# Four tokens to a row for r at the start of a fused RWKV and squared-ReLU kernel

## The chip, the cores and the metric

The kernel runs on one core of a Trainium2 chip. The metric is the device time of one execution in microseconds. Most executions of one kernel agree within 0.3%.

## The reference

Inputs are `r`, `k`, `v` of shape (4 batches, 8 heads, 768 tokens, 48), `w` and `u` of shape (8, 48), and two weight matrices of 384x2048 and 2048x384, all float32. A linear recurrence runs over the tokens, and its result goes through a two-layer network with a squared ReLU:

```python
state = zeros((B, H, D, D))
for t in range(S):
    kt, vt, rt = k[:, :, t], v[:, :, t], r[:, :, t]
    cur = einsum('bhd,bhe->bhde', u[None] * kt, vt)
    y[:, :, t] = einsum('bhd,bhde->bhe', rt, state + cur)
    state = w[None, :, :, None] * state + einsum('bhd,bhe->bhde', kt, vt)
x = y.transpose(0, 2, 1, 3).reshape(B * S, H * D)
out = (maximum(x @ w_in, 0) ** 2) @ w_out
```

## The kernel before

The work is cut into 24 units: 6 chunks of 128 tokens times 4 batches, chunk by chunk, so units 0 to 3 are the first chunk. For each unit the kernel loads r, k and v with the 128 tokens on the partitions (`load`, line 278; tiles `ldr`, `ldk`, `ldv`), scales r by a power of w that depends on the token and k by the inverse power (`scale`, line 300, on DVE; tile `rkw`), turns both so that the features lie on the partitions (`turn` and `evict_rk` through PE and ACT for units 0 to 5, `turn_dma` for the others), multiplies them into two 128-token score matrices (`at`, line 337), masks these (`mask`, line 349, on DVE), and forms y from the masked scores and the running state (`y_mm`, lines 400 and 406). `sums` adds the outer products of k and v and the diagonal term with u; `diag_v` and `evict_y` bring the diagonal term and y together. y is turned (`x_turn` with `evict_x`, or `x_dma`) and goes through `mm1` (line 447), `relu`, `square` and `mm2` (line 471); `evict_o` and `store` write it out.

The powers of w come from a spread of log w to all partitions (`spread_log`, PE, out of the one-row tile `wrow`), and an exponential with one exponent for each partition (`power`, ACT). `spread_columns` and `copy_columns` bring w and u to columns, from which `u_columns` and `end_columns` make small constants on POOL. `fill` is a matmul of constants whose result nobody reads.

Nothing is ordered by a scheduler at run time. A list of words, `SCHEDULE`, says in which order the steps are issued; each step appends its instructions to its engines' queues, and every engine works its own queue in order. A number behind `@` is the PSUM bank of the step, and `3*fill` is three fills. The loads of units 2 to 5 go to POOL's DMA queue, together with the two weight matrices, each in four quarters (`weights`, lines 285 to 291); the other loads, and the transposes by DMA, go to SP's. The first quarter of w_in waits on POOL for k of unit 0, by a small copy into `gate`. Buffers for the loads are handed out in the order of the list from pools of 3 (r), 8 (k) and 4 (v). The list starts:

```python
load:0:kt fill@0 load:0:rt 2*fill load:1:rt 2*fill load:1:kt fill columns 2*fill spread_log@1 load:0:vt load:2:rt
load:1:vt weights:kt.0:0:I fill power:0 3*fill load:2:kt power:1 scale:0:0 load:6:kt fill spread_columns@2 scale:1:0
load:2:vt fill load:9:kt scale:0:1 2*fill copy_columns turn:0:0@3 load:3:rt fill evict_rk:0:0 turn:0:1@4 u_columns
```

Of the kernel before, what the change touches and what calls it, by code (L numbers as in the profile page):

```python
# [8 lines left out]
F32 = mybir.dt.float32  # L9
BF16 = mybir.dt.bfloat16  # L10
AF = mybir.ActivationFunctionType
# [6 lines left out]
load:0:kt fill@0 load:0:rt 2*fill load:1:rt 2*fill load:1:kt fill columns 2*fill spread_log@1 load:0:vt load:2:rt  # L18
load:1:vt weights:kt.0:0:I fill power:0 3*fill load:2:kt power:1 scale:0:0 load:6:kt fill spread_columns@2 scale:1:0
load:2:vt fill load:9:kt scale:0:1 2*fill copy_columns turn:0:0@3 load:3:rt fill evict_rk:0:0 turn:0:1@4 u_columns  # L20
fill evict_rk:0:1 fill scale:2:0 turn:1:0@5 load:3:kt fill rk:0 at:0@6,7 scale:1:1 weights:-:1:I fill mask:0:0 fill
turn:1:1@1 cast_v:0 weights:-:2:I mask:0:1 fill evict_rk:1:0 fill load:7:kt fill load:3:vt evict_rk:1:1 y_mm:0@2
2*fill sums:0@3 load:4:rt fill diag_v:0 turn:2:0@4 end_columns rk:1 at:1@6,7 evict_rk:2:0 evict_y:0 2*fill scale:2:1
2*fill x_turn:0@5 mask:1:1 6*fill mask:1:0 3*fill turn:2:1@1 scale:3:0 fill weights:-:3:I evict_rk:2:1 3*fill
scale:3:1 2*fill evict_x:0 fill turn:3:0@4 load:5:rt rk:2 cast_v:2 fill at:2@2,7 load:6:rt fill mask:2:0 fill
weights:-:0:O fill mm1:0:1:0@6 state_add:0 load:4:kt turn:3:1@1 relu:0:1:0 3*fill mask:2:1 fill cast_v:1 mm1:0:1:1@5
weights:-:1:O evict_rk:3:0 sums:1@2 state_cast:0 fill load:4:vt diag_v:1 sums:2@3 y_mm:1@6 relu:0:1:1 y_mm:2@7
evict_y:1 fill mm1:0:1:2@4 evict_rk:3:1 load:5:vt diag_v:2 fill rk:3 x_turn:1@5 at:3@6,1 evict_x:1 evict_y:2
load:5:kt fill relu:0:1:2 fill mask:3:0 3*fill cast_v:3 mm1:1:1:1@5 square:0:1:1:0 square:0:1:0:1 load:8:kt sums:3@7
mask:3:1 x_turn:2@4 mm1:1:1:0@6 evict_x:2 diag_v:3 relu:1:1:1 y_mm:3@1 state_add:1 weights:-:2:O mm1:2:1:2@4  # L30
relu:1:1:0 square:0:1:2:1 evict_y:3 mm1:2:1:1@5 square:1:1:0:1 state_add:3 weights:-:3:O mm1:2:1:0@6 state_add:2
x_turn:3@2 fill evict_x:3 mm1:2:1:3@1 scale:4:0 relu:2:1:2 fill mm1:1:1:3@7 relu:2:1:1 square:2:1:2:1 square:2:1:1:0
mm1:0:1:3@3 relu:2:1:0 mm1:3:1:1@2 square:2:1:0:1 mm1:3:1:3@4 relu:3:1:1 scale:4:1 mm2:1:0@5 square:1:1:1:1
relu:1:1:3 turn:4:0@6 mm2:0:0@2 relu:0:1:3 load:7:rt mm1:1:1:2@7 relu:2:1:3 evict_rk:4:0 fill turn:4:1@3 fill
mm1:3:1:0@1 evict_rk:4:1 cast_v:4 rk:4 mm2:1:1 scale:5:0 relu:1:1:2 at:4@6,0 relu:3:1:0 mm2:2:0@3 mask:4:1
state_cast:2 turn:5:0@7 mask:4:0 sums:4@1 square:1:1:2:1 mm2:0:1 scale:5:1 evict_rk:5:0 diag_v:4 y_mm:4@0 mm2:2:1
evict_y:4 turn:5:1@6 scale:6:1 mm2:0:2 evict_rk:5:1 state_add:4 square:3:1:0:1 x_turn:4@7 mm2:2:2 square:0:1:3:0
evict_x:4 square:3:1:1:1 at:5@0,6 load:6:vt mm2:3:0@1 state_cast:3 mask:5:1 mm1:4:1:0@7 square:1:1:3:0 load:8:rt
state_cast:1 rk:5 mm2:3:1 cast_v:5 mask:5:0 relu:3:1:3 mm2:0:3 square:2:1:3:0 mm1:4:1:3@6 scale:6:0 mm2:2:3
relu:4:1:3 turn_dma:6 relu:4:1:0 sums:5@0 y_mm:5@4 diag_v:5 mm1:4:1:2@6 load:8:vt scale:7:1 evict_y:5 mm1:4:1:1@7  # L40
relu:4:1:2 scale:7:0 square:4:1:0:1 mm2:1:2 state_decay:4 turn_dma:7 square:4:1:3:0 x_turn:5@4 mm2:1:3 evict_x:5
square:3:1:3:0 relu:4:1:1 mm2:4:0@6 load:7:vt evict_o:0 square:4:1:1:0 mm1:5:1:3@4 store:0:POOL load:9:rt scale:8:0
mm2:4:1 relu:5:1:3 scale:8:1 load:10:rt evict_o:1 rk:6 at:6@7,2 square:4:1:2:1 mm1:5:1:1@4 mask:6:1 cast_v:6
turn_dma:8 mm1:5:1:0@5 mask:6:0 relu:5:1:1 state_add:5 mm2:4:2 relu:5:1:0 square:5:1:1:1 mm1:5:1:2@2 sums:6@4
relu:5:1:2 mm2:4:3 diag_v:6 square:5:1:0:1 state_decay:5 y_mm:6@7 cast_v:7 rk:7 at:7@5,0 evict_y:6 square:5:1:2:1
mm2:5:0@2 mask:7:1 x_dma:6 mm1:3:1:2@7 state_add:6 mm2:5:1 relu:3:1:2 load:10:kt mask:7:0 load:9:vt sums:7@0
square:3:1:2:1 scale:9:1 mm2:5:2 evict_o:4 diag_v:7 y_mm:7@4 state_cast:4 store:4:POOL scale:9:0 at:8@7,5 evict_y:7
cast_v:8 turn_dma:9 mm2:3:2 store:1:POOL rk:8 mm1:6:1:0@6 square:5:1:3:0 x_dma:7 scale:10:0 sums:8@4 relu:6:1:0
mm2:5:3 state_add:7 mm1:6:1:1@6 evict_o:5 load:11:kt state_decay:6 square:6:1:0:1 mask:8:1 load:11:rt mm1:6:1:3@0
state_cast:5 scale:10:1 mm2:6:0@2 mask:8:0 state_cast:6 mm2:3:3 diag_v:8 turn_dma:10 relu:6:1:1 y_mm:8@5 relu:6:1:3  # L50
mm1:6:1:2@7 evict_y:8 cast_v:9 square:6:1:1:0 x_dma:8 at:9@6,0 relu:6:1:2 mm1:7:1:1@5 rk:9 square:6:1:2:1
square:6:1:3:0 sums:9@7 load:12:rt evict_o:2 mm2:6:1 mask:9:1 relu:7:1:1 load:10:vt store:2:POOL mask:9:0 mm2:6:2
# [505 lines left out]
```

## Time and profile before

| | |
|---|---|
| median of 3 runs | 177.45 us (177.1 to 177.91) |
| the profiled execution's own time | 176.95 us |
| its span, first to last instruction | 175.1 us |
| PE, DVE, ACT, POOL busy | 167.7, 128.8, 128.1, 33.2 us |
| fills on PE | 68 |
| DMA moved | 28.83 MB, mean 165 GB/s |
| packets under 512 B | 89681 of 93848 |

PE is TensorE's matmuls, PEld its weight loads, DVE VectorE, ACT ScalarE, POOL GpSimd, SP SyncE. The ends of matmuls are modelled and overlap the next one, so a busy PE is not PE at its peak. The granted clock is 1.00 in every stretch of the trace. SP's queue is `q1`, POOL's is `q0`, and `q10` carries the one load that ACT issues, that of w.

### The profile page before, as it was taken

The page shows a single profiled execution, that of the slowest core. Times are in us where ns is not written, and L with a number is a line of the kernel's source. Part 1 is how long each engine was busy: PE and PEld are TensorE (multiplying, and loading weights), DVE is VectorE, ACT ScalarE, POOL GpSimd, SP SyncE. Part 2 cuts the span into 40 slices and gives each one's busy share as a digit, 9 for nine tenths or more (in the row PEclk, how much of TensorE's full clock was granted, in tenths as well). Part 3 has the DMA queues.
Part 4 walks back from the last instruction along what each step waited for, and adds up shares of the span by engine and source line. Part 5 has one row for each costly group of instructions (what it writes and reads, how often), then busy time and mean ns, then how long its engine had stood idle before and what let it go on. Part 6 is the DMA issues. An engine that isn't in the chain of part 4 may idle for free.

```text
span 175.1 us, 4846 instructions
## 1 busy us (share of the span) xinstructions
PE 167.7 (96%) x1946; PEld 132.1 (75%) x1946; DVE 128.8 (74%) x280; ACT 128.1 (73%) x266; POOL 33.2 (19%) x66
## 2 busy tenths in 40 slices
PE   7869999999999999999999999999999999999992
PEld 3547999777787888696786886986886886878870
DVE  4459797199788998997998999689988497550400
ACT  4344798977787797799486989299498595992951
POOL 8998560000010203000201101010110011120010
PEclk9999999999999999999999999999999999999999
DMA  5999999978595999999999998998999987521013
GB/s 109 196 221 191 215 231 249 197 139 160 108 217 106 193 159 215 198 196 155 178 236 170 230 118 188 205 131 190 207 172 170 161 165 201 112 78 35 4 45 135
DMA packets 93848, 28.83 MB, mean 165 GB/s; under 512 B 89681, under 2 KB 91730, under 8 KB 93826
## 3 DMA queue, kind: packets, MB, share of 16 engines
q1 hardware_dynamic: 89472, 18.88, 63.5%
q0 software_dynamic: 4352, 9.64, 22.7%
q8 instruction: 15, 0.25, 0.6%
q14 instruction: 7, 0.06, 0.2%
q10 hardware_dynamic: 2, 0.00, 0.0%
HBM read 20.45 MB, written 4.72 MB: 144 GB/s over the span
## 4 chain that ended last, share of the span: by engine, by line
PE 76%; DMA 9%; ACT 6%; DVE 4%; SPq 2%; issue 1%; DVEq 0%
PE bank L447 31%; PE bank L471 30%; DMA ldv<-in_v_dram 4%; PE bank L337 4%; DMA rkT<-rkw 3%; PE bank L245 2%; PE bank L400 2%; PE bank L362 2%; ACT gr L455 2%; DMA xT<-yb 2%; SPq L278 2%; PE bank L406 2%; PE bank L486 2%; ACT g L462 1%; DVE g L464 1%; ACT osb L478 1%
## 5 line engine op out<-in xcount | busy, mean ns | idle before, releaser
L447 PE MATMUL bank<-xT,w_in_q 128*128 128x128 bf16 (+1 forms) x768 | 72.4, 246 | 0.3 <-DMA xT<-yb 0.3
L455 ACT ACTIVATE gr<-bank 128x512 f32<-128x512 f32 x96 | 53.7, 603 | 20.2 <-PE bank L447 18.9
L471 PE MATMUL bank<-w_out_q,g 128*128 128x384 bf16 x368 | 68.5, 326 | 0.0
L447 PEld LDWEIGHTS <-w_in_q 128*128 128x128 bf16 x768 | 64.1, 114 | 3.6 <-issue 0.5
L471 PEld LDWEIGHTS <-g 128*128 128x128 bf16 x368 | 33.5, 98 | 18.4
L462 ACT ACTIVATE g<-gr 128x512 bf16<-128x512 f32 x60 | 37.0, 641 | 0.4
L505 POOL DMA_DIRECT2D out_dram<-osb x21 | 11.3, 542 | 131.5 <-ACT osb L478 120.3
L349 DVE TENSOR_TENSOR am<-bank,smask 128x512 bf16<-128x512 f32 x48 | 31.5, 683 | 1.9 <-PE bank L337 1.5
L464 DVE TENSOR_TENSOR g<-gr 128x512 bf16<-128x512 f32 x36 | 24.5, 685 | 9.9 <-ACT gr L455 9.7
L371 DVE TENSOR_TENSOR dv<-vb,bank 128x384 f32<-128x384 bf16 x24 | 13.2, 549 | 7.5 <-PE bank L362 4.6
L300 DVE TENSOR_TENSOR rkw<-ldr,wpos 128x384 bf16<-128x384 f32 x24 | 13.2, 551 | 5.2 <-DMA ldr<-in_r_dram 2.6
L415 DVE TENSOR_TENSOR yb<-bank,dv 128x384 bf16<-128x384 f32 x24 | 13.3, 554 | 4.8 <-PE bank L406 4.1
L391 ACT CAST stb<-st 64x192 bf16<-64x192 f32 x40 | 13.9, 349 | 2.4 <-DVE st L385 2.0
L304 ACT CAST vb<-ldv 128x384 bf16<-128x384 f32 x24 | 12.3, 513 | 3.8 <-DMA ldv<-in_v_dram 3.5
L478 ACT COPY osb<-bank 128x384 f32<-128x384 f32 x23 | 11.0, 486 | 5.5 <-PE bank L471 5.4
L245 PE MATMUL bank<-warm 128*128 128x256 bf16 x68 | 13.6, 315 | 1.2 <-DVE warm L193 1.2
L329 DVE TENSOR_TENSOR rk<-rkT 128x512 bf16<-128x512 bf16 x24 | 10.0, 419 | 5.8 <-ACT rkT L324 4.3
L300 DVE TENSOR_TENSOR rkw<-ldk,wneg 128x384 bf16<-128x384 f32 x24 | 13.2, 550 | 0.3 <-DMA ldk<-in_k_dram 0.3
L381 DVE TENSOR_TENSOR st<-bank,st 64x192 f32<-64x192 f32 x32 | 11.2, 351 | 0.2
L324 ACT COPY rkT<-bank 128x512 bf16<-128x512 bf16 x12 | 6.9, 585 | 6.0 <-PE bank L320 5.9
L400 PE MATMUL bank<-vb,am 128*128 128x48 bf16 x192 | 8.6, 183 | 1.4 <-ACT vb L304 1.4
L400 PEld LDWEIGHTS <-am 128*128 128x128 bf16 x192 | 7.8, 96 | 2.6 <-issue 1.4
(61 smaller groups left out, 115.6 us busy)
## 6 DMA issues: line engine op xcount, KB each, us to landing
out_dram<-osb POOLq DMA_DIRECT2D x21, 192.0 KB, 3.3
ldk<-in_k_dram SPq DMA_DIRECT2D x20, 192.0 KB, 4.0
ldr<-in_r_dram SPq DMA_DIRECT2D x20, 192.0 KB, 4.1
ldv<-in_v_dram SPq DMA_DIRECT2D x20, 192.0 KB, 4.0
w_in_q<-in_moe_w_in_dram POOLq DMA_DIRECT2D x4, 384.0 KB, 8.6
w_out_q<-in_moe_w_out_dram POOLq DMA_DIRECT2D x4, 384.0 KB, 11.4
ldr<-in_r_dram POOLq DMA_DIRECT2D x4, 192.0 KB, 8.4
ldk<-in_k_dram POOLq DMA_DIRECT2D x4, 192.0 KB, 8.7
```

Of the source, the lines that this page charges most:

```text
L245: nc.tensor.matmul(out=bank("fill")[:, :WIDE], lhsT=warm[:, :128], rhs=warm, start=True, stop=True)
L300: nc.vector.tensor_tensor(t["rkw"][:, x, :, :, :D], pair(src), pair(wx), ALU.mult)
L349: nc.vector.tensor_tensor(am, t["at"][o], smask.unsqueeze(1).to_broadcast([C, HP, C]), ALU.mult)
L371: nc.vector.tensor_tensor(t["dv"], t["vb"], t["d"].unsqueeze(2).to_broadcast([C, H, D]), ALU.mult)
L391: nc.scalar.copy(stb[b][sl, :, o * D : (o + 1) * D], st32[b][sl])
L400: nc.tensor.matmul(out=y[:, 2 * p + o, :], lhsT=t[f"am{o}"][:, p, :], rhs=t["vb"][:, 2 * p + o, :], start=(o == 0 and p == 0), stop=c == 0 ...
L415: nc.vector.tensor_tensor(t["yb"], t["y"], t["dv"].rearrange("p h d -> p (h d)"), ALU.add)
L447: nc.tensor.matmul(out=t["h", s][:, a], lhsT=turned, rhs=chunks[c]["xT"][:, n, b : b + m, :], start=(n == 0), stop=(n == NK - 1),)
L455: nc.scalar.activation(t["gr", s], t["h", s], AF.Relu)
L462: nc.scalar.activation(g, x, AF.Square)
L464: nc.vector.tensor_tensor(g, x, x, ALU.mult)
L471: nc.tensor.matmul(out=t["o"], lhsT=chunks[units[i][0]]["g"][:, f, units[i][1], :], rhs=w_out_q[f // 4][:, f % 4, :], start=(f == 0), stop ...
```

## The change

- **r of units 0 to 5.** A row of the tile is now four tokens of one head. Each load is two transfers, one for the even heads and one for the odd: partition 32a + s holds tokens 4s to 4s + 3 of head 2a + o. `scale` multiplies with a table in the same order (`packed_pos`), and `evict_rk` puts the tokens back into their order while it copies out of PSUM.
- **w.** It is loaded as four rows (`w4`) rather than one, and its logarithm is spread from these: once for the packed table (`spread_log:0`, then four exponentials of 96 columns, `power:0`), once for the plain tables (`spread_log:1`, `power:1`, and `power:2` later). The columns of w are copied from `w4` on DVE instead of being loaded again; u's load moves to SP.
- **Weights.** Each quarter comes in two pieces, and the pieces alternate on POOL's queue with r, k and v of units 1 to 5. The copy that made the first quarter wait for k of unit 0 is gone.
- **Engines and order.** `u_columns`, `end_columns` and a memset move from POOL to DVE; the two 128x128 constant masks stay on POOL but move behind the first loads of the list; v of unit 1 moves from SP to POOL. The pools are 5, 6 and 5 buffers. The whole list is in a new order.

The diff, without most of the list:

```diff
+load:0:kt fill@0 load:1:rt triangle 3*fill load:2:rt fill load:0:rt 3*fill identity copy_w spread_log:0@1 load:1:kt
+load:3:rt columns fill power:0 spread_log:1@2 load:0:vt weights:2:I:0 load:2:kt scale:0:0 fill power:1 fill
+scale:1:0 weights:0:I:1 2*fill scale:0:1 fill turn:1:0@3 load:1:vt load:6:rt scale:1:1 fill turn:0:0@4 scale:2:0
+weights:2:I:1 fill evict_rk:0:0 fill turn:0:1@5 scale:3:0 load:3:kt fill evict_rk:0:1 turn:1:1@6 evict_rk:1:0
+load:4:rt fill rk:0 at:0@7,1 evict_rk:1:1 fill load:5:rt mask:0:0 fill spread_columns@4 load:6:kt mask:0:1
+weights:3:I:1 fill cast_v:0 scale:2:1 2*fill load:2:vt at:1@5,3 copy_columns rk:1 u_columns fill cast_v:1
+weights:0:I:0 fill end_columns sums:0@6 load:4:kt mask:1:1 y_mm:0@7 fill turn:2:0@1 diag_v:0 fill evict_rk:2:0 fill
+weights:1:I:1 fill load:7:kt fill mask:1:0 fill turn:2:1@4 power:2 sums:1@3 load:3:vt load:8:rt scale:3:1 fill
+evict_rk:2:1 3*fill y_mm:1@1 evict_y:0 2*fill weights:1:I:0 at:2@5,2 diag_v:1 fill mask:2:0 fill weights:3:I:0 fill
+x_turn:0@4 turn:3:0@7 evict_x:0 evict_y:1 2*fill load:4:vt fill evict_rk:3:0 2*fill mask:2:1 2*fill cast_v:2 3*fill
+state_add:0 weights:2:O:1 3*fill x_turn:1@5 fill evict_x:1 y_mm:2@4 load:5:kt rk:2 turn:3:1@1 scale:4:0 fill
+evict_rk:3:1 mm1:0:1:0@7 weights:1:O:0 scale:5:0 sums:2@2 relu:0:1:0 scale:4:1 turn:4:0@6 weights:0:O:0 fill
...
-    wrow = const.tile([1, dm], F32)
-    nc.scalar.dma_start(out=wrow, in_=w.rearrange("h d -> (h d)").unsqueeze(0))
+    J = 4
+    w4 = const.tile([HP, 2, D], F32)
+    nc.scalar.dma_start(out=w4, in_=w.rearrange("(p o) d -> p o d", o=2))
...
+    select = const.tile([HP, HP, 32], F32)
+    nc.vector.tensor_copy(select, ident4.unsqueeze(2).to_broadcast([HP, HP, 32]))
+    spread_p = const.tile([HP, HP, 128], F32)
+    nc.vector.tensor_copy(spread_p, ident4.unsqueeze(2).to_broadcast([HP, HP, 128]))
+    shift = const.tile([128, J], F32)
+    for n in range(4):
+        for j in range(J):
+            nc.vector.memset(shift[32 * n : 32 * n + 32, j : j + 1], float(j - C * n - C // 2))
+    packed_up = const.tile([128, J], F32)
+    nc.vector.scalar_tensor_tensor(packed_up, iota_i.to_broadcast([128, J]), float(J), shift, ALU.mult, ALU.add)
...
+        if x == 0:
+            for j in range(J):
+                nc.scalar.activation(
+                    packed_pos[:, j].rearrange("p o d -> p (o d)"), spread["log", 0][:, : 2 * D], AF.Exp,
+                    scale=packed_up[:, j : j + 1],
+                )
...
-        (nc.gpsimd if i in (2, 3, 4, 5) else nc.sync).dma_start(
-            out=x, in_=src[b, :, c * C : (c + 1) * C, :].rearrange("h s d -> s h d")
-        )
+        queue = nc.gpsimd if i in (2, 3, 4, 5) or name + str(i) in ('vt1',) else nc.sync
...
+        if name == "rt" and i < NPE:
+            for o in range(2):
+                queue.dma_start(
+                    out=x[:, o * J : (o + 1) * J, :].rearrange("p j d -> p (j d)"),
+                    in_=src.rearrange("(a o) (s j) d -> o a s (j d)", o=2, j=J)[o],
+                )
+        else:
+            queue.dma_start(out=x, in_=src.rearrange("h s d -> s h d"))
...
-    def weights(after, q, which):
-        if after is not None:
-            nc.gpsimd.tensor_copy(gate, tiles[after[1]][after[0]][:, 0, :1])
+    def weights(q, which, part):
         if which == "I":
...
+            sl = slice(0, 2) if part == 0 else slice(2, NK)
+            nc.gpsimd.dma_start(out=w_in_q[q][:, sl, :], in_=src[:, sl, q * dff // NQ : (q + 1) * dff // NQ])
...
-        nc.scalar.copy(t["rkT"][:, x], t["tp", x])
+        if x == 0:
+            nc.scalar.copy(
+                t["rkT"][:, 0].rearrange("q a (s j) -> q a s j", j=J), t["tp", 0].rearrange("q j (a s) -> q a s j", a=HP)
+            )
+        else:
+            nc.scalar.copy(t["rkT"][:, 1], t["tp", 1])
```

More of the change, by code (lines that the diff above doesn't have):

```diff
@@ L17 @@
 SCHEDULE = """
[L18 to L52, printed above, removed]
@@ L145 @@
     const = ctx.enter_context(tc.tile_pool(name="const", bufs=1))
[L146 to L148 removed]
+    room = {'ldr': 5,
+            'ldk': 6,
+            'ldv': 5,
             'rkw': 4,
```

221 lines of the change are left out of this document (128 added, 93 removed).

## The prediction

> **What bounds the kernel now.** I read the page first, then the stages, PE's waits and the start instruction by instruction.
>
> ```profile
> span 175.1 us, 4846 instructions
> PE 167.7 (96%) x1946; PEld 132.1 (75%) x1946; DVE 128.8 (74%) x280; ACT 128.1 (73%) x266; POOL 33.2 (19%) x66
> ...
> PE   7869999999999999999999999999999999999992
> ...
> DMA  5999999978595999999999998998999987521013
> ```
>
> From the third slice on, PE has no visible hole until the last one. The stages of the start say more:
>
> ```profile
> 0.00:4.00 4.00, 2.75 (x10) 1.53 (x10) 2.17 (x18) 1.80 (x2) 3.20 (x15) 1.00 0.53 100
> 4.00:8.00 4.00, 3.46 (x17) 1.89 (x16) 1.66 (x4) 1.05 (x2) 4.00 (x6) 1.00 1.13 197
> 8.00:12.00 4.00, 3.08 (x31) 2.12 (x29) 2.69 (x5) 1.28 (x3) 3.89 (x8) 1.00 1.22 230
> 12.00:16.00 4.00, 3.23 (x48) 2.58 (x48) 2.59 (x6) 1.96 (x4) 3.44 (x10) 1.00 1.16 179
> 16.00:20.00 4.00, 4.00 (x60) 3.53 (x58) 3.70 (x8) 2.44 (x6) 3.55 (x5) 1.00 1.22 209
> ```
>
> The columns are PE, PEld, DVE, ACT and POOL busy, granted clock, DMA share and GB/s. PE is full from 16 us, and the DMA engines are full (share above 1) from 4 us on. What PE does before 16 us is mostly fill:
>
> ```profile
> 9.75 0.40 PE L337 MATMUL bank<-rkT 64*128 64x128 bf16 x8
> ...
> 15.00 1.15 PE L245 MATMUL bank<-warm 128*128 128x256 bf16 x9
> ...
> 18.06 0.83 PE L447 MATMUL bank<-xT,w_in_q 128*128 128x128 bf16 x12
> ```
>
> The row at 9.75 is `at:0`, the one at 18.06 the first `mm1`, 8.3 us later. Nine fills take 1.15 us, one of them 0.27 in flight, so a fill costs (1.15 - 0.27)/8 = 0.11 us. Since PE does not stop after about 16 us, the whole time is the moment of the first `mm1`, plus the PE work that still stands behind it, plus the waits there. That is my sum. The PE waits of the first 40 us are short:
>
> ```profile
> PE bank L400 <- ACT vb L304: 1.4, 1, 1.4
> ...
> PE bank L258 <- DMA wu<-in_w_dram: 0.5, 1, 0.5
> ```
>
> So the waits that a better start could take away come to 1.9 us in these two. The profiled execution took 176.95 us, 1.85 outside its span; the median of the runs is 177.45, 0.5 above it. I make the sum as a difference and add it to the median.
>
> **The change, part by part.** *PE work behind the first `mm1`.* Both lists hold 68 fills and the same matmuls of weight size. Counted in the two lists, 52 fills stand ahead of the first `mm1` before and 56 after, and `turn:3:1`, `y_mm:1`, `y_mm:2`, `sums:1` and `x_turn:1` move ahead of it.
>
> ```profile
> 14.82 0.34 PE bank L431 x3
> ...
> 16.14 0.22 PE bank L320 x4
> ...
> 20.31 0.19 PE bank L362 x4
> ...
> 20.88 0.40 PE bank L400 x16
> ```
>
> A turn is 0.22, two y products 0.40, sums about 0.2 to 0.3, x_turn below 0.34: about 1.0 us, and four fills 0.44. So the first `mm1` may come 1.5 us later at no cost: term one, -1.5.
>
> *The r loads.* Before, a load is 1024 runs of 192 B, with the 128 tokens as the outermost extent on both sides. After, each r load of units 0 to 5 is two transfers of 128 runs of 768 B, whose source counts 4 pairs of heads, then 32 rows. How a transfer is dealt to engines decides its price. The trace has both ends:
>
> ```profile
> q1 hardware_dynamic: 1743, 0.33, 108.4%
> ...
> q10 hardware_dynamic: 2, 0.00, 3.4%
> ```
>
> The first row is the window 2.2 to 3.8 us, where only SP's 128-row loads run: all 16 engines busy, 1.6 x 16 x 1.084 / 1743 = 16 ns for a 192 B packet. The second is 1.60 to 1.75 us, the load of `wrow`, whose outermost extent is one: two packets, so one of data on one engine (the other marks the end), 0.15 x 16 x 0.034 = 0.08 us for 1.5 KB. The engines used follow the outermost extent at both ends. A half of r has an outermost extent of 4 on one side; I take four engines for it, 24.6 KB on each. At `wrow`'s rate a half is 1.3 us, at the 192 B rate (128 x 16 ns) 2.0 us, and if it did spread over sixteen it would be a quarter of these or less, 0.3 to 0.5. I take 1.3, the row with the longer run. Nothing in this trace shows whether successive transfers on SP take the same four engines; I take that they do. The Trainium skill (DMA: Bandwidth & Descriptors, Rules for kernel authors, "Use all 16 engines") says so: the engine count comes from the slowest dimension larger than one, and an outermost extent below 16 confines the transfer to that many. By the same page's section on why a DMA increments its semaphore by 16, SP's queue always takes the lowest-numbered ones, so these four halves would run one after the other; no run here shows that yet.
>
> What they stand behind and in front of on SP's queue:
>
> ```profile
> L278 SPq DMA_DIRECT2D ldk<-in_k_dram x1: 457/457/457, 0.7 to 0.7; - x1
> DMA to landing us min/median/max: 3.1/3.1/3.1
> ...
> L278 SPq DMA_DIRECT2D ldr<-in_r_dram x2: 567/682/797, 1.3 to 1.9; - x2
> DMA to landing us min/median/max: 3.9/4.1/4.2
> ...
> L278 SPq DMA_DIRECT2D ldk<-in_k_dram x1: 1305/1305/1305, 2.7 to 2.7; - x1
> DMA to landing us min/median/max: 4.8/4.8/4.8
> ...
> L278 SPq DMA_DIRECT2D ldv<-in_v_dram x1: 706/706/706, 4.1 to 4.1; - x1
> DMA to landing us min/median/max: 7.8/7.8/7.8
> ```
>
> Before: k0 lands at 3.8, r0 at 5.2, r1 at 6.1, k1 at 7.5, v0 at 11.9. v0 came 4.4 us after k1, although the earlier loads follow each other by 1.0 to 1.4: sharing with POOL's r2 and weights cost it 3. After, the order is k0, r1, r0, k1, u, v0. Four halves at 1.3 put r0 at 3.8 + 5.2 = 9.0 and k1 at 10.0 if nobody else were there; POOL, now without the copy that held its weights for k0, feeds r2, r3 and pieces of w_in into the same engines from about 4 us. With some 2 of v0's 3 us, k1 lands at 12. Bounds: 6.5 (sixteen shares, half price) to 14.
>
> *From k1 to `at:0`.* `at:0` now stands behind `turn:1:1` on PE, which needs `scale:1:1`, which needs k1. That is a scale and a turn with hand-over: 12 + 0.55 + 0.6 gives `at:0` at 13.2 against 9.75. Everything behind `scale:0:0` and `scale:1:1` on DVE waits with them (the scales of units 2 and 3, the masks), and `load:4:rt` on POOL waits for r1's buffer, with the weights behind it. In the other bound DVE's four scales in a row from 5.4 put `at:0` at 9.2.
>
> *From `at:0` to the first `mm1`.* DVE has in this stretch six masks, two scales, two dv, two yb, one rk, and a copy of the columns, then ten small operations that POOL did before.
>
> ```profile
> 5.42 0.56 DVE L300 TENSOR_TENSOR rkw<-ldr,wpos 128x384 bf16<-128x384 f32 x1 [2.39 <-ACT wpos L253]
> ...
> 7.09 0.16 DVE L261 COPY cols<-bank 128x8 f32<-128x8 f32 x1
> ...
> 10.25 1.29 DVE L349 TENSOR_TENSOR am<-bank,smask 128x512 bf16<-128x512 f32 x2
> 13.41 0.55 DVE L371 TENSOR_TENSOR dv<-vb,bank 128x384 f32<-128x384 bf16 x1 [1.87 <-ACT rkT L324]
> 13.88 0.42 DVE L329 TENSOR_TENSOR rk<-rkT 128x512 bf16<-128x512 bf16 x1
> 14.21 0.55 DVE L415 TENSOR_TENSOR yb<-bank,dv 128x384 bf16<-128x384 f32 x1
> ...
> L218 DVE MEMSET rkw<- 128x64 uint32 x8 | 0.6, 112 | 0.0
> ...
> L291 POOL DMA_DIRECT2D w_out_q<-in_moe_w_out_dram x4 | 2.3, 567 | 1.2 <-DMA w_in_q<-in_moe_w_in_dram 1.0 <-issue 0.2
> ```
>
> That is 6 x 0.645 + 6 x 0.55 + 0.42 + 0.16 + 10 x 0.13 = 9.05 us; the small ones lie between 0.08 (eight memsets in 0.6) and 0.16 (the copy). With `y_mm:2`, `turn:3:1`, a fill and hand-overs (0.8) it is 9.9 against 8.3 before: +1.6, bounds +1.1 to +2.0. Term two is then (13.2 - 9.75) + 1.6 = +5.1.
>
> *At nothing.* The sixteen one-column memsets, the two copies of the small identity and the packed exponents add about 2 us to DVE's preparation, covered by r0's landing; in the sixteen-share case they end about when the four 96-column exponentials do. The 96-column spreads replace one of 384 at the same total. The reordered copy out of PSUM reads 128x512 as before; I keep ACT's price and bound it by twice, hidden while ACT waits for PE. The sixteen memsets are priced by the eight above. The weight pieces add eight POOL issues of 0.57 us (the last row), under the transfers already queued. The new buffers and the reordering after 40 us I count as +0.4 between -1 and +1.5, since PE had no slack to gain there.
>
> Sum: -1.5 + 5.1 + 0.4 = +4.0, so 181.5 us.
>
> **The rivals.** *The packing works as meant.* The halves spread over sixteen engines (or over different fours at once), k1 lands at 6.5, `at:0` at 9.2, and POOL's load of v1 ends the late v. Then -0.55 + 1.1 - 1.5 and a start without the late vb (up to 1.4 of waiting) give about -1.2: 176.2. For it: 768 B runs cut 1024 packets to 256 where the DMA share is above 1. The same page of the skill, in its specifications, wants runs of at least 512 B for line rate, which would favour this case. Against it: the row of `wrow`. It decides from r0 and r1 landing by about 6. *Starved.* r0 and k1 get through only once POOL's queue has run dry at `load:4:rt`, held for r1's buffer: k1 at 16 rather than 12, 185.5. For it: v0's 7.8. *Hidden.* Four engines, but at half price and with little sharing, k1 at 9.5: 2.5 less at `at:0`, and the smaller prices of the small operations (-0.5) and no loss later (-0.4) leave +0.6; with the late vb gone (-0.4) it is 177.6.
>
> **How the numbers follow.** Four engines with sharing 0.62; works as meant 0.18; starved 0.10; hidden 0.10. About 0.5% is what a measurement of this kernel tells from no change. Faster is the second case, 0.18; same is the last, 0.10; slower the other two, 0.72. Four shares with k1 between 10 and 14 give 179.5 to 183.5, with the other bounds 178 to 185. The range leaves out the case that works as meant and the end of the starved one, and takes in the hidden one: 176.8 to 186.
>
> **What would show it.** In the profile after: the r loads on SP landing at 7 us or later where they took 4.1; DVE's first scale waiting for ldr, not for the exponentials; PE idle before its first turn; `at:0` near 13, the first `mm1` near 23; DVE gapless from there; the load of w, now four rows, leaving a few packets on its queue, not 16 or more; PE full from then on. I am wrong if the scale of unit 0 starts before 6.5 us, or if the time lost at the first `mm1` is given back behind it.

## The result, and the profile after

| | before | after |
|---|---|---|
| median | 177.33 us (177.1 to 177.91, 4 runs) | 188.62 us (188.32 to 189.8, 4 runs) |
| ratio | | 1.0644 [1.0591, 1.0696] |
| profiled execution, span | 176.95, 175.1 us | 188.6, 186.8 us |
| `scale:0:0` / `at:0` / first `mm1` start at | 5.42 / 9.75 / 18.06 us | 15.66 / 19.63 / 30.64 us |
| span behind the first `mm1` | 157.0 us | 156.2 us |

Medians are of all executions of a run; a ratio leaves out those more than 1.5% above the fastest of their kernel.

The change makes the kernel slower by 6.4%. The forecast was slower by 2.3%, 181.5 us; the measured time lies above its range. The page of the changed kernel:

```profile
span 186.8 us, 4913 instructions
...
PE   7504799999999999999999979999999999999992
...
PEclk9999969999999999999999999999999999999999
DMA  2996999994079996999996999699999796622023
```

A slice is 4.7 us. PE now has a hole in the second, third and fourth slices, where the kernel before had one shallow start; from the sixth slice on the two are alike. The stretches of the start show what stood still (columns as in the prediction):

```profile
8.00:12.00 4.00, 0.00 (x0) 0.00 (x0) 0.00 (x0) 0.00 (x0) 1.95 (x3) 1.00 1.20 221
12.00:16.00 4.00, 0.00 (x0) 0.00 (x0) 0.34 (x1) 0.00 (x0) 0.00 (x0) 1.00 0.78 159
16.00:20.00 4.00, 3.25 (x29) 2.65 (x29) 3.08 (x7) 1.70 (x4) 3.48 (x6) 1.00 0.74 146
20.00:24.00 4.00, 2.76 (x43) 1.90 (x38) 3.52 (x14) 1.27 (x3) 3.35 (x5) 0.91 1.32 186
24.00:28.00 4.00, 4.00 (x46) 3.19 (x45) 3.56 (x9) 1.65 (x3) 3.35 (x5) 0.66 1.20 224
```

From 8 to nearly 16 us PE, DVE and ACT do nothing at all, while the DMA share is 1.20 from 8 to 12. The engines wait for data, and the DMA engines move mostly other data. Which data DVE waits for stands in its timeline:

```profile
3.97 0.13 DVE L254 COPY wu<-w 4x96 f32<-4x96 f32 x1
15.66 1.03 DVE L341 TENSOR_TENSOR rkw<-ldr,packed_pos 128x384 bf16<-128x384 f32 x2 [11.56 <-DMA ldr<-in_r_dram]
...
17.31 0.56 DVE L341 TENSOR_TENSOR rkw<-ldk,wneg 128x384 bf16<-128x384 f32 x1 [0.15 <-DMA ldk<-in_k_dram]
...
22.31 0.16 DVE L297 TENSOR_TENSOR cols<-cols 128x4 f32<-128x4 f32 x1
22.50 0.45 DVE L300 CAST uwb<-cols 64x4 bf16<-64x4 f32 x2
22.97 0.16 DVE L303 TENSOR_TENSOR wend_c<-cols 128x4 f32<-128x4 f32 x1
23.17 1.15 DVE L305 TENSOR_TENSOR wend_c<-wend_c 128x4 f32<-128x4 f32 x6
```

The bracket is the idle time before the instruction and what ended it: 11.56 us for r. The scale at 17.31 is `scale:1:1`; k1 landed only then. The chain of work that ended last puts the same 12 us on one transfer (start, duration, what):

```profile
3.19 12.35 DMA ldr<-in_r_dram
```

PE's timeline has the two marks of the sum, and fills that cost twice what they did:

```profile
16.75 0.61 PE L361 MATMUL bank<-identb,rkw 128*128 128x128 bf16 x4 [9.55 <-DVE rkw L341]
...
19.63 0.49 PE L383 MATMUL bank<-rkT 64*128 64x128 bf16 x8
...
20.60 0.50 PE L263 MATMUL bank<-warm 128*128 128x256 bf16 x3
...
24.20 1.27 PE L263 MATMUL bank<-warm 128*128 128x256 bf16 x5
...
30.64 0.83 PE L493 MATMUL bank<-xT,w_in_q 128*128 128x128 bf16 x12
```

The span grew by 11.8 us: 10.2 at the first scale, -0.4 from there to `at:0` (3.97 against 4.33), 2.7 from `at:0` to the first `mm1` (11.01 against 8.31), -0.8 behind it. A single fast fill shows 0.27 and a slow one 0.42 in flight. So the three fills at 20.60 cost (0.50 - 0.27) / 2 = 0.115 us each, about as before, and the five at 24.20 cost (1.27 - 0.42) / 4 = 0.21, where the granted clock is low. PE's longest waits:

```profile
PE bank L361 <- DVE rkw L341: 9.6, 1, 9.6
PE bank L403 <- DVE uwb L300: 1.2, 1, 1.2
PE bank L493 <- DMA xT<-yb: 1.2, 2, 1.1
```

### The profile page after: what moved, and what is told of

Read it like the earlier page. It is cut to its first block, busy times and chain, and to the rows that moved or that the text cites. A ratio compares the mean times of both kernels' runs of the same rounds, so it can differ in the third digit from the quotient of the medians.

```text
span 186.8 us, 4913 instructions
## 1 busy us (share of the span) xinstructions
PE 170.2 (91%) x1954; PEld 135.4 (72%) x1954; DVE 132.0 (71%) x310; ACT 128.9 (69%) x270; POOL 36.2 (19%) x65
## 4 chain that ended last, share of the span: by engine, by line
PE 83%; DMA 11%; DVE 3%; SPq 1%; issue 1%; ACT 0%; DVEq 0%
PE bank L493 34%; PE bank L517 29%; DMA ldr<-in_r_dram 7%; PE bank L383 4%; DMA xT<-yb 4%; PE bank L263 4%; PE bank L446 3%; PE bank L361 2%; PE bank L408 2%; PE bank L452 2%; PE bank L532 1%; PE bank L403 1%; SPq L314 1%; DVE am L395 1%; DVE yb L461 1%
## 5 line engine op out<-in xcount | busy, mean ns | idle before, releaser
L517 PE MATMUL bank<-w_out_q,g 128*128 128x384 bf16 x368 | 67.0, 326 | 0.0
L517 PEld LDWEIGHTS <-g 128*128 128x128 bf16 x368 | 34.1, 98 | 19.2
L395 DVE TENSOR_TENSOR am<-bank,smask 128x512 bf16<-128x512 f32 x48 | 32.3, 686 | 7.1 <-PE bank L383 6.7
L508 ACT ACTIVATE g<-gr 128x512 bf16<-128x512 f32 x60 | 36.3, 637 | 0.5
L263 PE MATMUL bank<-warm 128*128 128x256 bf16 x68 | 15.5, 331 | 1.2 <-DVE warm L196 1.2
L361 PE MATMUL bank<-identb,rkw 128*128 128x128 bf16 x48 | 6.1, 266 | 9.6 <-DVE rkw L341 9.6
L366 ACT COPY rkT<-bank 128x512 bf16<-128x512 bf16 x6 | 3.5, 590 | 14.6 <-PE bank L361 14.6
L361 PEld LDWEIGHTS <-rkw 128*128 128x128 bf16 x48 | 4.5, 122 | 10.5 <-DVE rkw L341 10.0
L341 DVE TENSOR_TENSOR rkw<-ldr,packed_pos 128x384 bf16<-128x384 f32 x6 | 3.1, 553 | 11.6 <-DMA ldr<-in_r_dram 11.6
```

The source lines that it names most:

```text
L263: nc.tensor.matmul(out=bank("fill")[:, :WIDE], lhsT=warm[:, :128], rhs=warm, start=True, stop=True)
L341: nc.vector.tensor_tensor(t["rkw"][:, x, :, :, :D], a, b, ALU.mult)
L361: nc.tensor.transpose(t["tp", x][:, p, :], t["rkw"][:, x, p].rearrange("p o e -> p (o e)"), identb)
L395: nc.vector.tensor_tensor(am, t["at"][o], smask.unsqueeze(1).to_broadcast([C, HP, C]), ALU.mult)
L508: nc.scalar.activation(g, x, AF.Square)
L517: nc.tensor.matmul(out=t["o"], lhsT=chunks[units[i][0]]["g"][:, f, units[i][1], :], rhs=w_out_q[f // 4][:, f % 4, :], start=(f == 0), stop ...
```

## The experiments

All times in the table are from the profiled execution but the median and its ratio to the kernel before. The span behind the first `mm1` is 155 to 158 us in every run, so a run is decided mostly by what its start does.

| run | first scale | `at:0` | first `mm1` | span | median | ratio, 95% |
|---|---|---|---|---|---|---|
| before | 5.42 | 9.75 | 18.06 | 175.1 | | |
| after | 15.66 | 19.63 | 30.64 | 186.8 | 188.62 | 1.0644 [1.0591, 1.0696] |
| r0, r1 in four transfers of extent 32 | 9.17 | 13.14 | 25.16 | 181.8 | 184.47 | 1.039 [1.0313, 1.0466] |
| POOL's weights held for r0 | 12.08 | 16.05 | 29.26 | 187.5 | 189.38 | 1.069 [1.0639, 1.0741] |
| no packing, rest kept | 7.17 | 11.14 | 21.68 | 178.4 | 180.52 | 1.0201 [1.0145, 1.0256] |
| all r in four transfers | 6.76 | 10.74 | 26.81 | 183.6 | 186.12 | 1.0506 [1.0432, 1.058] |
| tokens outermost (4s + a) | 7.07 | 11.04 | 21.28 | 177.5 | 179.35 | 1.0132 [1.0103, 1.0161] |
| the same, three list edits | 4.99 | 10.48 | 24.12 | 179.3 | 181.02 | 1.0214 [1.019, 1.0238] |
| all POOL loads held for r0 | 9.56 | 15.22 | 31.23 | 189.3 | 191.08 (one run) | |
| no packing, columns on POOL | 6.22 | 10.20 | 24.79 | 181.0 | 181.87 | 1.0263 [1.0242, 1.0283] |
| tokens outermost, r0 first | 5.02 | 10.15 | 21.55 | 177.4 | 178.9 | 1.0093 [1.0062, 1.0124] |
| the same, columns later | 5.14 | 10.49 | 21.34 | 177.5 | 179.08 | 1.0119 [1.0075, 1.0162] |
| the same, r2 held | 4.85 | 9.90 | 24.51 | 181.2 | 183.0 | 1.0325 [1.0296, 1.0355] |
| r0 first, weight piece 0:I:0 earlier | 5.14 | 10.42 | 22.53 | 178.2 | 179.85 | 1.0151 [1.0133, 1.0169] |
| the same, `y_mm:2` behind | 5.06 | 10.86 | 20.91 | 176.7 | 178.51 | 1.0073 [1.0048, 1.0099] |
| r0 first, `y_mm:2` behind alone | 5.17 | 11.05 | 22.94 | 178.9 | 179.88 | 1.0139 [1.0094, 1.0184] |
| kernel before, packed with 4s + a | 4.86 | 9.75 | 17.12 | 175.0 | 176.76 | 0.9959 [0.9934, 0.9984] |
| the same, quarter 1 earlier | 4.86 | 9.75 | 17.34 | 175.3 | 177.22 | 0.9997 [0.998, 1.0014] |

One thing differs beside the edits. In the profiled executions of the changed kernel and of seven runs PE's granted clock falls to 0.50 in the first 36 us, for about 3.4 us or twice that by its means over stretches of 2 us; in the others, and before, it is 1.00 there. The seven are the two with POOL held for r0, all r in four transfers, the three list edits, no packing with the columns on POOL, r2 held, and `y_mm:2` behind alone. But for the run with POOL's weights held, where it falls behind the first `mm1`, a late first `mm1` of these can hold a part that is not the edit's. What sets it off is not shown. For the changed kernel it does not carry the result: two executions with a mean clock of 1.00 took 188.32 and 188.63 us.

My theory was the prediction's: an r half whose outermost extent is 4 runs on four DMA engines and shares them with POOL's traffic. The rivals were that the packing costs nothing and the rest of the change does, and that POOL's new stream alone starves SP.

**No packing.** All r loads as before, everything else as changed.

```diff
-        if name == "rt" and i < NPE:
-            for o in range(2): ...
+        queue.dma_start(out=x, in_=src.rearrange("h s d -> s h d"))
```

> The changed kernel, its list, buffers, weight pieces and engines, but r of units 0 to 5 loaded plainly in one transfer each, with the plain table and the plain copy out of PSUM; the plain table's exponential comes before the first scale and the spread for the packed table is left out. Theory 1: r0 and r1 land by 6.5, DVE's first scale at 6.5 to 7, time 178 (176.5 to 180.5). Theory 2: POOL's flood still holds SP's loads, 183 or more. Theory 3: 185 or more, since list and DVE work are unchanged.

```profile
7.17 1.03 DVE L331 TENSOR_TENSOR rkw<-ldr,wpos 128x384 bf16<-128x384 f32 x2 [2.76 <-DMA ldr<-in_r_dram]
```

The top of the expected range: 180.52. The first scale is 8.5 us earlier than after, and the whole span 8.4 us shorter: the packing costs 8.4 of the 11.8 us, all of it before the first scale. The other 3.3 us belong to the rest of the change.

**r0 and r1 in four transfers by pair of heads,** so that each counts 32 rows outermost.

```diff
-            for o in range(2): ... out=x[:, o*J:(o+1)*J, :] ... "(a o) (s j) d -> o a s (j d)"
+            if i < 2:
+                for a in range(HP): ... out=x[32*a : 32*a+32] ... "(a o) (s j) d -> a s o (j d)"
```

> The changed kernel, but r of units 0 and 1 (SP's queue) is loaded in four transfers by pair of heads, outermost extent 32 on both sides, instead of two with an outermost extent of 4. Same runs of 768 B, same layout. Theory 1 (an outermost extent of 4 confines a half to four DMA engines, on SP's queue always the same four, where POOL's traffic then starves it): r0 lands at 7 to 8 us, held only by eight issues of 0.6 us, DVE's first scale starts near 8 rather than 15.7, the first mm1 near 23, the time is 181 (179 to 183.5). Theory 2 (the engines are not the point; POOL's flood without the old hold starves everything that SP loads): no gain, 187 to 190. Theory 3 (the new list and the work moved to DVE cost the time): no gain, 187 to 190.

```profile
9.17 1.03 DVE L348 TENSOR_TENSOR rkw<-ldr,packed_pos 128x384 bf16<-128x384 f32 x2 [5.06 <-DMA ldr<-in_r_dram]
```

6.5 us of the first scale come back, bytes and run length being the same; the extent changed, and with it the number of transfers. The time, 184.47, is above what I expected, though single executions lie from 183.25 to 186.42. The halves of r2 and r3 on POOL still had extent 4, and SP now issued eight transfers for r; what each costs was not taken apart.

**POOL's weights held for the first half of r0** by a small copy on POOL that reads it.

```diff
-load:0:vt weights:2:I:0
+load:0:vt hold:0 weights:2:I:0
```

> The changed kernel with one small POOL copy that makes the first piece of the weights, and all that POOL issues behind it, wait for r of unit 0. Theory 1: r0 still takes 128 packets of 36 ns on four engines beside r2, so DVE's first scale starts at 10 to 11 us; first mm1 near 25.5, time 183.5 (182 to 185.5). Theory 2: without the flood r0 lands at about 6, time 178 to 180. Theory 3: no gain.

```profile
12.08 1.03 DVE L346 TENSOR_TENSOR rkw<-ldr,packed_pos 128x384 bf16<-128x384 f32 x2 [7.96 <-DMA ldr<-in_r_dram]
```

r came 3.6 us earlier, so sharing is part of the price; the time did not follow (189.38, expected 183.5), since POOL's queue is in order and all that stands behind the copy came later: the first weight piece was issued at 10.63 us, not 5.36. PE waited there for a v:

```profile
PE bank L451 <- ACT vb L350: 1.9, 1, 1.9
```

**All POOL loads held until r0 had landed.** This measures the confined transfer by itself.

```diff
-load:2:rt fill load:0:rt 3*fill
+fill load:0:rt hold:0 load:2:rt 3*fill
```

> The changed kernel with everything that POOL loads held until both halves of r of unit 0 have landed, so that SP's queue is alone on the DMA engines at the start. It measures the price of the halves by themselves; the time of the kernel is no matter, since POOL's loads come late (190 or more). Theory 1: k0 until 3.0, then 128 packets of 36 ns on each of the same four engines: r0 lands at 8.5 to 9.5, first scale there, and the 768 B packets run at some 110 per us. If successive transfers used different engines, or all, they would run at 200 to 440 per us and the first scale would start at 6 or before.

```profile
4.00:5.00 1.00, 1.00 (x6) 1.00 (x5) 0.12 (x2) 0.82 (x4) 0.00 (x0) 1.00 0.24 73
...
7.00:8.00 1.00, 0.20 (x1) 0.00 (x0) 0.00 (x0) 0.00 (x0) 0.00 (x0) 1.00 0.28 83
```

```profile
9.56 1.03 DVE L346 TENSOR_TENSOR rkw<-ldr,packed_pos 128x384 bf16<-128x384 f32 x2 [5.43 <-DMA ldr<-in_r_dram]
```

In these two stretches hardly anything but r moves, several halves of it queued, and the DMA share is 0.24 and 0.28: 3.8 and 4.5 engines of 16. 73 to 83 GB/s are 95 to 108 runs of 768 B per us. What moves between the two stretches fixes the count, by the trace's single packets. From 5 to 7 us 764 packets of 192 B pass beside r's 236. k1 has 1024 such packets, and twelve sixteenths of them are 768, if it is spread evenly over the engines. Hardly any more pass until 8 us, when r is nearly through. So each half holds four engines, all four halves the same four, and a quarter of k1 waits behind them. The page DMA: Bandwidth & Descriptors of the Trainium skill (Why a DMA increments its semaphore by 16 and not by 1), on which the prediction leaned without a row, has it so, the lowest-numbered engines included; these rows agree with the count and the queueing, and do not show which four they are. The first scale at 9.56 is what the prediction had for r0 undisturbed (9.0, and a hand-over). Beside POOL it is 15.66: sharing costs 6.1 us.

**How the sharing works.** The DMA queues of the changed kernel (packets, MB, share of 16 engines), q0 being POOL's and q1 SP's. The first row is from 5 to 6 us, the next two from 10 to 12, the last two from 12 to 13:

```profile
q1 hardware_dynamic: 116, 0.08, 27.5%
...
q0 software_dynamic: 301, 0.42, 104.5%
q1 hardware_dynamic: 79, 0.06, 14.6%
...
q0 software_dynamic: 129, 0.22, 97.2%
q1 hardware_dynamic: 32, 0.01, 6.7%
```

From 10 to 12 us SP's 79 packets, r's halves but for a few, are 19.8 on each of four engines, and POOL's 301 are 18.8 on each of sixteen, if both are dealt evenly, which is not shown. By that count about one r packet passes for each POOL packet, though these are larger (0.06 MB against 0.42), and a turn is 2 us / 19.8 = 0.10 us. The same page of the Trainium skill (SWDGE vs HWDGE vs iDMA) says that an engine goes round its queues, GpSimd's and the others' being different ones; the count agrees in this stretch.

The turn is not the same throughout. While POOL had moved little, from 5 to 6 us, 116 packets passed on SP's queue; from 12 to 13 it was 32, of 0.01 MB. By the trace's single packets three of the four halves had passed at 9.65 us, 6.7 us after the first packet, and the last one took until 14.64. So 128 packets per engine at 0.10 us, 12.9 us, meet the chain's 12.35 only as an average. Why the last half was so slow, one of its four engines behind the others perhaps, is not shown.

**All six r in four transfers.**

```diff
-            for o in range(2): ... "(a o) (s j) d -> o a s (j d)"
+            for a in range(HP): ... "(a o) (s j) d -> a s o (j d)"
```

> As the first of these, with r of all six units in four transfers by pair of heads, also on POOL's queue. Theory 1: the start as in the first, but POOL issues 24 transfers for four loads where it issued 8 of 0.68 us, so its weights and k come 5 us later at most: 181 to 184. Theories 2 and 3: 187 to 190.

```profile
6.76 1.03 DVE L341 TENSOR_TENSOR rkw<-ldr,packed_pos 128x384 bf16<-128x384 f32 x2 [2.65 <-ACT wneg L286]
...
14.20 0.56 DVE L341 TENSOR_TENSOR rkw<-ldk,wneg 128x384 bf16<-128x384 f32 x1 [1.67 <-DMA ldk<-in_k_dram]
```

```profile
PE bank L403 <- DVE uwb L300: 2.9, 1, 2.9
```

The start is repaired: the first scale no longer waits for r. But sixteen issues on POOL where there were eight push k2 back (the scale at 14.20 waits for it), and the columns and v behind it: 186.12, above the range. What was saved at the start came back, at least in part, as issue time on an in-order queue; PE's granted clock, 0.52 from 14 to 20 us, has a share in it that was not measured.

**Tokens outermost.** Row 4s + a instead of 32a + s: two transfers as in the change, the same 768 B runs, 32 outermost.

```diff
-in_=src.rearrange("(a o) (s j) d -> o a s (j d)", o=2, j=J)[o]
+in_=src.rearrange("(a o) (s j) d -> o s a (j d)", o=2, j=J)[o]
```

> The changed kernel with the same packing, still two transfers of 128 runs of 768 B for each r load, but a row p now holds tokens 4s to 4s + 3 of pair a with p = 4s + a, so the source counts 32 groups of tokens first and then 4 pairs: outermost extent 32 instead of 4. The selection for the spread, the exponents and the order of the copy out of PSUM follow. Theory 1 (an outermost extent of 4 confines a half to four engines): r0 lands by 5.5, DVE's first scale at 5.5 to 6.5 instead of 15.7, at:0 near 10, first mm1 20 to 21, time 178.5 (177 to 180.5), below the 180.5 of the kernel without packing. Rival (768 B rows from rows 192 KB apart are slow in themselves): 186 or more.

From 4 to 5 us SP's queue now moves (packets, MB, share):

```profile
q1 hardware_dynamic: 277, 0.19, 57.6%
```

The order of two dimensions takes 15.66 to 7.07 at the first scale and 188.62 to 179.35 in time, in the middle of what I expected; 277 packets in a us are over twice what four engines moved. That rules out the rival: the 768 B runs still come from rows of different pairs (these lie 288 KB apart, not the 192 that the text above has). The first scale came later than the 5.5 to 6.5 expected, r1 being ahead of r0; with r0 first it starts at 5.02, in a run below. Against plain loads the span is 0.9 shorter here, which the two ratios, 1.0132 and 1.0201, cannot tell from nothing.

**The rest of the change.** These runs look for its 3 us. First, with tokens outermost, three edits of the order: r0 ahead of r1, the column operations back on POOL, and `mm2:10:2` ahead of `mm1:12:2:0`, where PE had waited 1.2 us for xT.

```diff
-load:1:rt triangle 3*fill load:2:rt fill load:0:rt
+load:0:rt triangle 3*fill load:2:rt fill load:1:rt
...
-scale:16:0 mm1:12:2:0@0
+mm2:10:2 scale:16:0 mm1:12:2:0@0
...
-        nc.vector.tensor_tensor(cols[:, 1, :], ...), and the others of u_columns and end_columns
+        nc.gpsimd.tensor_tensor(cols[:, 1, :], ...)
```

> The one before, with r of unit 0 ahead of r of unit 1, the ten small column operations back on POOL, and one mm2 step of unit 10 moved ahead of the first mm1 of unit 12, where PE waited 1.2 to 1.6 us in all four experiments so far. Theory 1, with the small operations costing DVE 1.9 us ahead of the first mm1: first scale at 5.5, first mm1 near 18.5, span 174.5, time 176.3 (175 to 178). Rival (POOL gives the time back, since its in-order queue holds loads behind the columns): 178.5 to 180.5.

```profile
PE bank L405 <- POOL uwb L302: 4.1, 1, 4.1
```

```profile
14.03 0.53 POOL L327 DMA_DIRECT2D w_in_q<-in_moe_w_in_dram  x1 [1.44 <-DMA w_in_q<-in_moe_w_in_dram]
14.89 0.90 POOL L321 DMA_DIRECT2D ldv<-in_v_dram  x1 [0.32 <-DMA ldv<-in_v_dram]
15.81 0.21 POOL L299 TENSOR_TENSOR cols<-cols 128x4 f32<-128x4 f32 x1
```

The rival was right, and the time, 181.02, lies even above its range: the columns stand behind issues that themselves wait for earlier transfers to land. Then the column operations on POOL alone, without packing:

```diff
-        nc.vector.tensor_tensor(cols[:, 1, :], ...), and the others, in the run without packing
+        nc.gpsimd.tensor_tensor(cols[:, 1, :], ...)
```

> The kernel without packing (180.5) with the ten small column operations back on POOL and nothing else changed. Theory: on DVE they take 1.9 us between the first two masks and the next, in a stretch where DVE has no hole, so the first mm1 comes 1.5 to 2 us earlier: 178.7 (178 to 179.5). Rival (PE waits there for something else, or POOL's loads behind them come late): 180 to 181.

```profile
PE bank L393 <- ACT vb L335: 3.1, 1, 3.1
```

Again no gain, 181.87; the three of its four executions with a mean clock of 1.00 took 181.5 to 182.0. In this list the columns on DVE, dear as they are, are no loss. Now they stay there, with the two other edits kept:

```diff
-load:1:rt triangle 3*fill load:2:rt fill load:0:rt
+load:0:rt triangle 3*fill load:2:rt fill load:1:rt
```

> The changed kernel with 4s + a as the row (as in the run with tokens outermost), r of unit 0 issued on SP ahead of r of unit 1, and the one matmul group mm2:10:2 moved ahead of mm1:12:2:0; the small column operations stay on VectorE. Theory (the time is that of the first mm1 plus about 155.3 of span behind it; the order of two loads is worth about 2 us of the start; the column operations on GpSimd were what spoilt the run that had them there): first scale 5.0, at:0 about 9.8, first mm1 20.0 to 20.8, span 175.3 to 176.1, time 177 to 178, no difference from the kernel before. Rival (v0 or the weights on GpSimd's queue are late whatever is done on SP): first scale 5.0 but first mm1 at 21.3 as without the new order, time 178.5 to 179.3.

```profile
6.95 6.86 DMA ldv<-in_v_dram
...
14.10 0.89 POOL ldv L321
14.98 6.52 DMA w_in_q<-in_moe_w_in_dram
```

The first scale came 2 us earlier, as expected, and the first `mm1` not at all (21.55 against 21.28); the time, 178.9, cannot be told from 179.35. The chain into the first `mm1` (start, duration, what) says why: POOL stands until an earlier v has landed, and the weight piece behind it, 0:I:0, lands just as the `mm1` starts.

```diff
-fill end_columns sums:0@6 ... state_add:0
+fill sums:0@6 ... end_columns state_add:0
```

> The kernel with r of unit 0 first, and end_columns (seven small products on VectorE, about 1.3 us) moved in the list from before sums:0 to just before state_add:0, where their result is first used. Theory (the chain at:0 to first mm1 runs through VectorE): first mm1 0.5 to 1.3 us earlier than with r of unit 0 first alone, time 176 to 177.3. Rival (the matmuls between at:0 and mm1 wait for v0 and w, not for VectorE): first mm1 within 0.3 us of the run without the move, time the same within 0.5.

No gain, 179.08: the rival. In this list, with the loads as they are, the seven products on DVE are not what the first `mm1` waits for.

```diff
-load:2:rt fill load:1:rt
+hold load:2:rt fill load:1:rt
```

> The kernel with r of unit 0 first and end_columns later, and in it GpSimd's first load (r of unit 2) held by a small copy that reads k of unit 0, so that the first three loads of SP run alone. Theory (what is on the queues in the first 5 us sets the start): k0, r0 and r1 land about 0.5 us earlier, first scale 4.5 to 5, at:0 0.5 earlier; but GpSimd's r2 is issued at about 5 where it was at 1.9, so at:2 and its rk are later, beyond the first mm1's need; time 175.5 to 177.5, at best 0.5 per cent faster than the kernel before. Rival (GpSimd's later loads and weights are late by what r2 is held, as in the run that held all weights): first scale 4.5 to 5, but first mm1 0.5 to 1 later than without the hold, time 177.5 to 178.5.

```profile
13.99 0.56 DVE L348 TENSOR_TENSOR rkw<-ldk,wneg 128x384 bf16<-128x384 f32 x1 [1.39 <-DMA ldk<-in_k_dram]
```

Slower than either expected, 183.0. The hold put POOL's first load off by 1.7 us, and k2 with it (this scale was at 12.41 without the hold), so k2's load had no slack. That is 1.6 us. The first `mm1` is 3.2 us later than without the hold, and PE's granted clock is 0.50 from 14 to 20 us; all five executions have a mean clock of 0.98, so the rest can be the clock's. Next I moved the piece that the chain had named, and then `y_mm:2`, which the new list puts ahead of the first `mm1`:

```diff
-load:4:rt ... weights:0:I:0 fill end_columns
+weights:0:I:0 load:4:rt ... fill end_columns
```

> The kernel with tokens outermost and r0 first, and in its list the weight piece 0:I:0 moved ahead of the loads of r of units 4 and 5 on GpSimd's queue, so that it is the fourth piece rather than the fifth and stands ahead of four r halves, one k and one v. Nothing else moves. Theory (the first mm1 needs both pieces of quarter 0, and the second of them was issued at 14.98 and landed at 21.5): it is issued at 9 to 10 and lands at 15.5 to 17; the first mm1 is then held by VectorE's chain and the late columns and v: 19.8 to 20.8, span 175.6 to 176.6, time 177.2 to 178.2 (178.9 without). Rival (the columns, v and VectorE hold the first mm1, and the piece only lands with it): first mm1 within 0.3 us of 21.55, time 178.6 to 179.2.

```profile
14.63 6.79 DMA ldv<-in_v_dram
...
21.44 0.52 ACT vb L347
```

A miss, 179.85: with the piece early, the chain goes through the next late load on POOL, v of unit 2, which `y_mm:2` needs.

```diff
-evict_x:1 y_mm:2@4 load:5:kt ... mm1:0:1:2@5
+evict_x:1 load:5:kt ... mm1:0:1:2@5 y_mm:2@4
```

> The kernel with the weight piece 0:I:0 earlier, and y_mm:2 moved in the list from behind evict_x:1 to behind mm1:0:1:2. Theory (two loads on GpSimd hold the first mm1 of this list, the piece 0:I:0 and v of unit 2; with the one early and the other's user behind, VectorE's chain is left): first mm1 at 19.8 to 20.6; y_mm:2 then waits for v until about 22, behind 1.6 us of work, so a part of the gain stays: span 176.0 to 177.0, time 177.7 to 178.7 (179.85 without the move). Rival (the wait only moves behind the first mm1): first mm1 at about 20 but the span behind it longer by as much, 157 to 158, time 179.3 to 180.

> The kernel with tokens outermost and r0 first, and y_mm:2 moved behind mm1:0:1:2, the weight pieces left as they are. Theory (the piece 0:I:0 holds the first mm1 by itself): first mm1 stays at 21.3 to 21.7, time 178.4 to 179.2 (178.9 without the move). Rival (v of unit 2 alone held it): first mm1 at 20 to 20.6, time 177.6 to 178.2.

```profile
5.41 9.60 DMA ldv<-in_v_dram
...
15.03 0.52 ACT vb L347
```

```profile
16.00:18.00 2.00, 2.00 (x19) 1.63 (x17) 2.00 (x5) 1.07 (x2) 2.00 (x4) 0.50 1.06 194
```

With both edits the time is 178.51, as expected, and 1.3 us less than with the piece alone; the first `mm1` at 20.91 is a little later than expected. The second edit alone gave 179.88, but its six executions fall in two groups: three at 178.75 to 179.05, inside the theory's range, and three at 180.71 to 181.54. The profiled one is of the latter three, so its first `mm1` at 22.94 says nothing of the others. The rows are its chain, where a third load, v of unit 0 on SP, landed late, and its granted clock; how the two share the difference is not shown. None of the six bears out the rival, that v of unit 2 alone held the first `mm1`. So several loads land within a us or two of each other ahead of the first `mm1`, each covers the next, and which is last differs from kernel to kernel. Against the run with r0 first, 178.9, the two edits together gain nothing that the intervals can tell.

**The packing alone, on the kernel before.** Its list, queues and whole weight pieces; only r packed with 4s + a, with the tables and steps that the packing needs.

```diff
-out=x, in_=src[b, :, c * C : (c + 1) * C, :].rearrange("h s d -> s h d")
+out=x[:, o*J:(o+1)*J, :] ..., in_=src.rearrange("(a o) (s j) d -> o s a (j d)", o=2, j=J)[o]
```

> The kernel before, with its own list, queues, whole weight pieces and column operations on GpSimd, and only the packing of r put in, with 4s + a as the row (outermost extent 32): r of units 0 to 5 in two transfers of 128 runs of 768 B, w spread from four rows, the exponentials for packed r, the reordering copy out of PSUM. Theory (packing spread over the engines takes traffic away at the start, 1024 packets of 16 ns to 256 of about 36 ns for each r load, 0.45 us of all engines each; the loss of the change lay in the confinement and in the rest of its order): first scale at 5.0 to 5.5 as before, v0 0.5 to 1 earlier, so that the 1.4 us of waiting for vb shrinks; first mm1 17.2 to 18, time 176.2 to 177.2, at best 0.5 per cent faster. Rival (the preparation that packing adds on VectorE and ScalarE, some 3 us, is not hidden in this list): first scale at 6 to 7, first mm1 18.5 to 19.5, time 177.8 to 178.8.

```profile
PE bank L487 <- DMA w_in_q<-in_moe_w_in_dram: 0.9, 2, 0.5
```

176.76 us, 0.4% under the kernel before, the interval just clear of no change: the best of all runs. PE's 1.4 us for vb are gone and the first `mm1` comes 0.94 us earlier; 0.9 of that goes to weights that are now late.

```diff
-load:3:kt fill rk:0 at:0@6,7 scale:1:1 weights:-:1:I
+weights:-:1:I load:3:kt fill rk:0 at:0@6,7 scale:1:1
```

> The kernel before with the packing (4s + a), and quarter 1 of w_in moved ahead of k of unit 3 on GpSimd's queue. Theory (PE waits 0.9 us for quarters 1 and 2 behind the first mm1): half of that wait goes, first mm1 as before at 17.1, time 176.2 to 176.6. Rival (the DMA engines are full, so the piece lands as late, or k3 is late in its place): time 176.7 to 177.1, no difference.

```profile
PE bank L355 <- DVE rkw L335: 0.9, 1, 0.9
```

The rival, a little above its range: 177.22, and PE waits the same 0.9 us for k of unit 3, which gave way.

## Why the prediction was wrong in size

- **The sum's form held.** The time is the first `mm1` plus a nearly fixed rest: +12.6 at the first `mm1`, -0.8 behind it, +11.8 of span.
- **Four engines held.** Four engines per half, halves one after the other, r0 at 9.0 if undisturbed: 9.56 measured with POOL silent. A few packets for w, DVE waiting for ldr, PE idle before its first turn, PE full later: all as listed. `at:0` near 13 and the first `mm1` near 23 were not.
- **The step that failed is the sharing,** "With some 2 of v0's 3 us, k1 lands at 12". It took v0's delay, that of a transfer on all engines, for one on four. There sharing cost 6.1 us (9.56 against 15.66 at the first scale), and k1 landed at 17.3, beyond the bound of 14. r packets and POOL's larger ones take turns there, by the count from 10 to 12 us; that this alone makes the 6.1 us is argued, not shown. The "starved" case had k1 at 16 and 185.5, nearest to what came, and its chance of 0.10 was too small. Its mechanism, r getting through only once POOL has run dry, fits at most the end: all but 17 of r's 512 packets had passed by 13 us, and in the us before that POOL's queue still moved 129.
- **From k1 to `at:0`** the path was wrong too. The prediction goes through k1 and `scale:1:1`. The chain goes from r0's landing at 15.54 through the first scale to PE, which works without a gap from 16.75 to `at:0`: four turns at 0.43 and five fills at 0.21. `scale:1:1` ended at 17.87, and PE came to `turn:1:1` only at 18.85. In five other runs with r1 first (no packing, r0 and r1 in four transfers, POOL's weights held, all r in four transfers, tokens outermost) `at:0` also comes 3.97 or 3.98 us after the first scale. With k1 at 12 the prediction had r0 at about 11.0, and 2.2 more led to `at:0`. So of the 6.4 us that `at:0` came late, some 4.5 are r0's landing and 1.9 are this path. A turn was priced at 0.22, a row from after 16 us; before `at:0` it is 0.43 in the kernel before as well.
- **`at:0` to the first `mm1`** 11.0, forecast 9.9. The ten column operations took 1.9 us rather than 1.3 (rows from 22.31 to 23.17: 0.16 + 0.45 + 0.16 + 1.15), above both rows that priced them, memsets and a copy. But the chain has DVE only up to `uwb`, three of the ten. From 23.0 on it is PE's row without a gap, not DVE's sum, and from there to 27 us PE runs at the lower clock. At the prices after 27 us that row would be some 1.5 us shorter, an estimate from the chain's rows, and the stretch about 9.5. That the sum came near by another path is luck.
- **Behind the first `mm1`** -0.8, forecast -1.5 + 0.4. Close, with a new wait of 1.2 us for xT that I had not named.
- **At nothing** held where it could be seen: DVE's preparation ended at 4.1 us, long before r, and the reordering copy out of PSUM takes what the plain one does:

```profile
L366 ACT COPY rkT<-bank x6: 585/588/601, 18.0 to 39.8; 128x512 bf16<-128x512 bf16 x6
```

- **The rivals.** "Works as meant" (176.2) fell with the four engines. Its figure is near that of the other order of dimensions on the old list, 176.76; on the new list, for which it was worked out, that order took 179.35.

What stays open is where most of the 3 us lie that the rest of the change costs. r0's place, the columns, a weight piece and `y_mm:2` were undone one by one, and 178.51 is the least that the new list gave; its longer row of PE and DVE work ahead of the first `mm1`, which the prediction priced at 1.6 on DVE, was not taken apart further.

## What to carry to other kernels

Here longer runs helped only where the outermost extent of the transfer stayed large: the same 768 B runs took 188.62 us with 4 outermost and 179.35 with 32. A transfer confined to a few engines is priced badly by its bytes, or by the delay of one that is spread: beside POOL's traffic it took 12.35 us, where 435 of its 512 packets passed in 4 us with POOL silent. Its packets per engine times a turn with the other queue's packets is a guess to try, which met the sum here but not the course. And try an idea alone on the old order first: here it was worth 0.4%, and the new order around it cost about 3 us.

## What the runs showed that I had not expected

- PE was slow twice, and the granted clock shows it once. Up to `at:0` a fill took 0.21 us at a granted clock of 1.00, here and in the kernel before (up to 9.4 us there). Between 20 and 21.7 us it was 0.11. From about 23.5 to 26.7 it was up to 0.21 again, with the granted clock at 0.91 and 0.66 in the stretches from 20 and 24 us; from 28 on it is 1.00 and a fill 0.11. PE had stood 9.55 us before its first turn and 1.24 before 23.0; which of them, if either, brought the second slow stretch is not shown.
- SP's queue blocks in the middle of a list of issues. u's load of 1.5 KB took 5.84 us to issue, behind r's halves and k1; why there is not shown:

```profile
5.24 5.84 SPq L251 DMA_DIRECT2D wu<-in_u_dram  x1
```
